# A fused sparse-attention and maxout kernel: fewer copies on GpSimd, another build of the distance table, another order of all units

## The chip, the cores and the metric

The kernel runs on one core of a Trainium2 chip. The metric is the time of one execution on the device, in microseconds. Three runs of the kernel before took 177.97, 178.1 and 178.21 us (median 178.1 us).

## What is computed

Inputs are q, k and v (4 batches, 8 heads, 768 positions, 64 per head, float32) and four weight matrices; the output is 3072 x 512 in float32.

```python
scores = scale * q @ k.T                       # per batch and head
keep   = (pos_k < 8) | (0 <= rel < 96)         # rel = pos_q - pos_k
dist   = where(global and not local, 96, |rel|)
scores = where(keep, scores - slope[h] * dist, -1e9)
a = softmax(scores);  x = concat_heads(a @ v)  # 3072 x 512
h = max(max(x @ w1, x @ w2), x @ w3)           # 512 -> 768
out = h @ w_out                                # 768 -> 512
```

A query sees the 96 positions up to its own and the first 8 positions of its batch. The slopes are 2^-1 to 2^-8 over the heads.

## The kernel before

The 3072 rows are 24 tiles of 128 queries, six to a batch. A tile works on a window of keys of its own and the tile before it (two sets of 128 keys, the global keys put into unused columns); the first tile of a batch has one set. Tiles come in seven chunks of 4, 2, 2, 4, 4, 4 and 4 for the two matrix layers, so a first-layer product is 512 or 256 columns wide.

The work is written as units, and the string SCHEDULE lists the units in the order in which they are issued. Each engine executes its part in that order, so the string fixes the order on every engine and on SP's DMA queue, and no scheduler changes it. A unit's last number often says which engine does its copy: 0 ScalarE (ACT), 1 VectorE (DVE), 2 GpSimd (POOL); in the transposes other numbers choose a pair of engines or a DMA. The units that matter here:

- l and v (load_part, load_v): load two tiles of Q or K, or of V, in float32, 512 KB. w and o load weight blocks. All but the first load of K are issued by SP.
- c (cast_part, L185) casts Q or K to bf16; C (cast_v, L188) casts half of a V pair; W (L489) and Q (L492) cast the weights.
- x (u_x): TensorE transposes of Q or K and the copy out of PSUM (L263 and L265; whole ones L282 and L284); how = 9 is a transpose by DMA (L249). In how 6 one half is copied by ScalarE and the other by VectorE, in 7 both by ScalarE, in 8 both by VectorE.
- Y (L192, L194): half copies of V into the key window's layout; Z (L205) copies the first keys; G (L230) and V (L192, L194) put the global keys and their V rows into the windows ("gathers" below).
- S (u_S): scores (L303) and their exponential on ScalarE (L314). For the first tiles a bias goes into the scores by a matmul (L296); for the others M (L330, L332) multiplies by a mask table on VectorE.
- A (u_A): product with V (L356) and division by the sums on VectorE (L360 to L369).
- T (u_XT): transposes of a tile's result (L397, L407, copies L400, L408), or by DMA (how = 4, L377).
- F (u_F1): one of three first-layer products (L420). F c.f.0 is copied by ScalarE (L425), F c.f.1 and F c.f.2 are a maximum on VectorE (L427, L429).
- O (u_F2) and E: second layer (L435), copy (L444), store.
- B and K build eight bias and eight mask tables from the distance table (L319 on ScalarE or VectorE; L323 on ScalarE). D issues dummy matmuls (L500).

PSUM has three buffers of one bank (psH) shared by F, O and some others, two double-bank score tiles (psS), and one bank for transposes (psT).

The distance table is built before the first unit: GpSimd counts positions into rbase (L509), VectorE makes the third set of keys, the condition and the maximum over all 384 columns (L514 to L521), and copies the table with its columns regrouped into rbq (L522). B reads rbq, K reads rbase.

Of the kernel before, what the change touches and what calls it, by code (L numbers as in the profile page):

```python
# [22 lines left out]


SCHEDULE = """
    D0.0 D7.0 D6.0 c0.0.2 D1.8 B0.0 B7.0 D9.4 D5.4 B3.1 B5.1 B4.1 l1.1 l1.0 c1.0.2 K3 K7 K4 K5 B1.0
    c0.1.1 x0.1.3 Z0.1 K1 B2.0 K6 B6.0 D3.4 K2 x0.0.6 S1.0.1 S1.1.1 G1.0 v0 C0.0.2 K0 c1.1.1 x1.1.8
    S0.0.1 x1.0.8 C0.1.2 Y1.0.1 S2.1.1 Y0.1.1 S2.0.1 G2.0 v1 V2.2 M1.0 M1.1 A1.2 Y0.0.1 M2.0 l2.0
    c2.0.1 C1.0.2 S0.1.1 M0.1 S3.0.1 M3.0 T1.8 C1.1.2 Y1.1.2 V3.2 S3.1.1 M3.1 G3.2 M0.0 A0.2 l2.1
    c2.1.2 x2.0.2 M2.1 A2.0 A3.1 Y2.0.2 T0.0 x2.1.7 T2.0 S4.0.1 w0.0 W0.0.2 w0.1 T3.8 l3.0 c3.0.1  # L30
    S4.1.0 M4.1 F0.0.0 W0.1.2 F0.0.1 G4.2 S5.0.0 S5.1.0 x3.0.8 F0.1.0 w0.2 V4.2 W0.2.2 M5.0 w1.0
    W2.0.0 v2 F0.0.2 C2.0.2 C2.1.2 W1.0.1 F0.1.1 F0.1.2 Y2.1.2 V5.2 M5.1 F0.2.0 F0.3.0 F0.4.0 w1.1
    W1.1.0 F0.5.0 W2.1.1 A5.0 M4.0 A4.1 F0.5.1 w1.2 W2.2.1 T5.0 F0.2.1 F0.4.1 T4.1 W1.2.0 l3.1
    F0.4.2 F0.5.2 c3.1.0 x3.1.6 Z1.2 l4.0 c4.0.0 F0.2.2 l4.1 v3 F1.2.0 F1.3.0 c4.1.1 l5.1 S7.0.0
    S6.1.0 C3.0.0 x4.0.6 C3.1.2 F1.2.1 F1.2.2 F1.4.0 F1.3.1 l5.0 o2 o1 F1.0.0 M7.0 o0 S7.1.0 S6.0.0
    c5.1.0 x4.1.6 v4 l7.0 F1.3.2 F1.4.1 l6.0 M7.1 F1.0.1 F1.4.2 v6 v5 F1.1.0 G7.2 A7.0 F1.5.0 F1.5.1
    l6.1 Q1.1 F1.1.1 F1.0.2 c5.0.0 S8.1.0 x5.0.6 S8.0.0 Q2.0 c7.0.0 Y3.0.0 F1.5.2 Q0.1 F0.3.1 M6.0
    F0.3.2 G8.2 Y3.1.2 Y4.0.2 M6.1 M8.0 F1.1.2 C4.0.1 l7.1 V8.2 S9.0.0 S9.1.0 G9.2 C4.1.2 x5.1.8
    O0.2.0 Y5.0.2 Y4.1.2 O1.0.0 C6.0.0 A6.0 O0.0.0 M9.1 T7.8 S10.1.0 S10.0.0 c6.0.0 c6.1.0 G10.0
    T6.8 M8.1 M9.0 V10.1 O1.1.1 M10.1 x6.1.9 C6.1.2 C5.0.2 V9.2 A8.1 Y7.0.2 F2.4.0 A9.0 x7.0.9  # L40
    F2.1.0 O0.1.0 M10.0 T9.4 F2.0.0 v7 T8.4 C5.1.0 l9.1 F2.4.1 S11.1.0 x6.0.8 S11.0.0 M11.1 Y5.1.2
    F2.1.1 F2.5.0 V11.2 O0.3.0 S13.1.0 c7.1.1 Z2.0 S13.0.0 x7.1.6 G13.1 F2.0.1 F2.0.2 l8.0 F2.5.1
    l9.0 l8.1 M11.0 F2.4.2 A10.1 F2.2.0 F2.2.1 A11.0 F2.3.0 F2.3.1 F2.5.2 F2.3.2 S12.0.0 T11.8 V14.2
    S12.1.0 F2.1.2 F2.2.2 S14.0.0 T10.6 S14.1.0 G14.2 Y6.0.0 O2.1.0 v9 M13.0 Y6.1.1 M14.0 F3.0.0
    M13.1 C7.0.1 C7.1.2 A13.1 F3.4.0 F3.1.0 M14.1 M12.1 c8.0.1 S15.1.0 S15.0.0 c8.1.0 Y7.1.1 v10
    T13.4 v8 Y8.0.1 O2.0.1 F3.3.0 F3.0.1 M15.1 F3.0.2 V15.0 C9.0.0 A14.1 V16.1 F3.1.1 M15.0 M12.0
    F3.2.0 F3.1.2 F3.4.1 F3.2.1 F3.3.1 F3.3.2 x8.0.9 x8.1.9 G15.2 c9.0.1 c9.1.0 x9.1.9 A12.0 C8.0.0
    C8.1.2 F3.5.0 F3.5.1 A15.1 F3.4.2 S16.0.0 x9.0.8 S16.1.0 M16.0 F3.2.2 F3.5.2 Z3.0 T15.6 G16.0
    l10.0 v11 T14.4 l10.1 S19.1.0 S19.0.0 O3.2.1 l11.1 O3.0.0 C10.0.2 C9.1.1 Y9.1.2 G19.2 Y8.1.2
    S17.1.0 T12.8 M19.1 S17.0.0 O3.1.0 M16.1 Y10.0.1 F4.1.0 A16.0 M17.0 F4.2.0 F4.0.0 c10.0.2  # L50
    x10.0.9 F4.0.1 c10.1.2 x10.1.9 F4.3.0 M19.0 M17.1 S18.1.0 S18.0.0 T16.4 l11.0 F4.0.2 A19.2 V17.2
    A17.1 F4.2.1 O3.3.0 T19.8 c11.1.0 S20.0.0 M18.1 M18.0 S20.1.0 G20.1 C11.0.1 F4.2.2 c11.0.2
    Y9.0.2 x11.0.9 C10.1.1 Y10.1.1 F4.4.0 F4.3.1 F4.5.0 A18.1 F4.1.1 F4.4.1 V20.0 S21.1.0 S21.0.0
    F4.4.2 G21.2 x11.1.9 C11.1.2 Y11.1.0 V23.0 F4.1.2 F4.5.1 T17.4 T18.4 F4.3.2 S22.1.0 M20.0 M20.1
    S22.0.0 G22.0 M22.1 F5.4.0 F5.4.1 F4.5.2 M21.1 F5.2.0 M21.0 A20.1 T20.4 F5.2.1 O4.2.1 F5.0.0
    F5.0.1 S23.0.0 M23.0 S23.1.0 F5.3.0 F5.2.2 V21.1 F5.1.0 M23.1 M22.0 F5.1.1 Y11.0.2 F5.3.1 V22.2
    A23.0 A22.2 T22.4 A21.1 O4.1.0 O4.3.0 T21.4 T23.4 F5.3.2 F5.4.2 F5.5.0 F5.5.1 O4.0.0 F5.0.2
    F5.1.2 F6.4.0 F6.1.0 F5.5.2 F6.1.1 F6.1.2 F6.3.0 F6.4.1 F6.4.2 F6.2.0 F6.5.0 F6.5.1 O5.0.0
    F6.5.2 F6.3.1 O5.1.1 O5.3.1 F6.0.0 F6.3.2 F6.2.1 F6.0.1 F6.2.2 F6.0.2 O5.2.0 E D4.1 D2.2 D8.0
"""  # L60


# [1 line left out]
def kernel(  # L64
# [437 lines left out]
    with tc.manual_schedule():  # L502
        load_part(0, 1)
        load_part(0, 0)

# [16 lines left out]
        nc.vector.tensor_copy(rbq.rearrange("p s (e i) -> p s e i", e=2), rbase.rearrange("p s (i e) -> p s e i", e=2))  # L522
# [43 lines left out]
```

## Time and profile before

| | |
|---|---|
| median of 3 runs | 178.1 us |
| the profiled execution | 178.15 us, of which the profile spans 176.4 us |
| busy: TensorE, VectorE, ScalarE, GpSimd | 169.0, 133.0, 109.2, 39.2 us |
| HBM read, written | 25.17 MB, 6.29 MB |
| TensorE clock granted | 1.0 |

The profile is one execution. Names of engines: PE is TensorE (PEld its weight loads), DVE VectorE, ACT ScalarE, POOL GpSimd, SP the engine that issues DMAs. Rows give line, engine, operation, output and inputs, count, busy microseconds and mean nanoseconds. Rows of stages give start and end, length, then busy time and count of PE, PEld, DVE, ACT and POOL, the clock, the DMA share and GB/s. Rows of the chain of waits give start, length and what stood on it. Rows in order of time give start, length, engine, line and operation. A few matmul records are missing.

### The profile page before, as it was taken

To read this page: it belongs to the slowest core of one execution; us is meant where nothing else is said; L and a number is where in the kernel's file an instruction comes from. 1 tells how busy PE (TensorE), PEld (TensorE's weight loads), DVE (VectorE), ACT (ScalarE), POOL (GpSimd) and SP (SyncE) were. 2 spreads that over 40 slices of the span, in tenths; PEclk is the share of its full clock that TensorE was granted. 3 is DMA by queue.
4 is the path that set the end of the run, shared out by engine and by line. 5 is a ranking of instruction groups with operands and counts; after the bars stand their busy time and mean duration, and the time that the engine had idled before them with its cause. 6 is when DMAs were issued, how large, how long until landed. Compare 5 with 4: busy or idle time off the path is not lost.

```text
span 176.4 us, 4322 instructions
## 1 busy us (share of the span) xinstructions
PE 169.0 (96%) x1695; PEld 94.0 (53%) x1717; DVE 133.0 (75%) x276; ACT 109.2 (62%) x170; POOL 39.2 (22%) x63
## 2 busy tenths in 40 slices
PE   7989899999999999999999999999999999999993
PEld 2445654558854668744545545444546444444452
DVE  7767796898999998996999598987969634534700
ACT  3998995769898988489625864669443222231042
POOL 2257845112076250020001280403000000000000
PEclk9999999999999999999999999999999999999999
DMA  4999999999999588999999398572030251003025
GB/s 126 346 309 331 364 350 382 385 351 383 288 290 302 192 207 180 278 299 277 228 227 284 88 259 144 164 152 30 0 89 4 59 149 61 4 32 117 29 92 205
DMA packets 53908, 35.54 MB, mean 201 GB/s; under 512 B 16768, under 2 KB 46336, under 8 KB 53888
## 3 DMA queue, kind: packets, MB, share of 16 engines
q1 hardware_dynamic: 52704, 34.68, 69.7%
q10 hardware_dynamic: 1184, 0.59, 1.2%
q8 instruction: 13, 0.21, 0.5%
q14 instruction: 7, 0.06, 0.1%
HBM read 25.17 MB, written 6.29 MB: 178 GB/s over the span
## 4 chain that ended last, share of the span: by engine, by line
PE 79%; DVE 8%; DMA 7%; POOL 2%; issue 2%; ACT 1%; SPq 0%; DVEq 0%
PE h L420 46%; PE po L435 15%; DMA rawv<-in_v_dram 7%; PE sp L303 5%; PE op L356 5%; PE wp L500 4%; DVE P L330 3%; PE tpr L258 2%; ACT P L314 1%; DVE qkT L265 1%; POOL vo L188 1%; DVE ht L429 1%; PE xtr L397 1%; DVE xT L400 1%; DVE wo L492 1%
## 5 line engine op out<-in xcount | busy, mean ns | idle before, releaser
L420 PE MATMUL h<-xT,w 128*128 128x512 bf16 (+1 forms) x492 | 99.4, 348 | 1.2 <-DVE xT L400 0.4
L420 PEld LDWEIGHTS <-w 128*128 128x128 bf16 x504 | 47.0, 98 | 41.5 <-issue 0.8
L314 ACT ACTIVATE P<-sp 128x1024 bf16<-128x1024 f32 (+1 forms) x48 | 43.7, 956 | 6.4 <-PE sp L303 5.9
L425 ACT CAST h<-h 128x512 bf16<-128x512 f32 (+1 forms) x42 | 22.0, 530 | 30.8 <-PE h L420 29.7
L435 PE MATMUL po<-wo,ht 128*128 128x512 bf16 (+2 forms) x146 | 33.2, 362 | 0.8 <-DVE ht L429 0.2
L429 DVE TENSOR_TENSOR ht<-h,h 128x512 bf16<-128x512 bf16 (+1 forms) x42 | 25.4, 608 | 10.4 <-PE h L420 8.9
L427 DVE TENSOR_TENSOR h<-h,h 128x512 bf16<-128x512 bf16 (+1 forms) x42 | 25.2, 606 | 9.1 <-PE h L420 8.5
L330 DVE TENSOR_TENSOR P<-P,wmask 128x1024 bf16<-128x1024 bf16 x33 | 23.8, 742 | 0.8 <-ACT P L314 0.6
L444 ACT COPY ost<-po 128x512 f32<-128x512 f32 (+2 forms) x19 | 10.5, 558 | 20.7 <-PE po L435 19.5
L435 PEld LDWEIGHTS <-ht 128*128 128x128 bf16 x156 | 14.3, 98 | 15.3 <-issue 0.5
L356 PEld LDWEIGHTS <-P 128*128 128x128 bf16 x352 | 13.2, 97 | 4.1 <-DVE P L330 0.7
L303 PE MATMUL sp<-qkT 64*128 64x128 bf16 x320 | 13.9, 217 | 0.5 <-DVE qkT L265 0.4
L369 DVE TENSOR_TENSOR xb<-op,rz 128x512 bf16<-128x512 f32 x20 | 13.8, 692 | 0.7
L303 PEld LDWEIGHTS <-qkT 64*128 64x128 bf16 x320 | 9.3, 94 | 8.1 <-issue 5.3
L185 POOL CAST qkp<-rawp 128x1024 bf16<-128x1024 f32 x6 | 7.4, 1248 | 15.0 <-DMA rawp<-in_q_dram 14.9
L444 DVE COPY ost<-po 128x512 f32<-128x512 f32 (+1 forms) x7 | 4.4, 632 | 8.1 <-PE po L435 8.1
L185 ACT CAST qkp<-rawp 128x1024 bf16<-128x1024 f32 x10 | 10.4, 1052 | 0.0
L188 POOL CAST vo<-rawv 128x512 bf16<-128x512 f32 x10 | 6.9, 702 | 15.5 <-DMA rawv<-in_v_dram 10.7
L500 PE MATMUL wp<-zeros 128*128 128x512 bf16 x23 | 7.9, 508 | 1.2 <-DVE zeros L513 1.2
L230 POOL COPY qkT<-qkT 128x32 bf16<-128x32 bf16 x9 | 2.5, 278 | 25.7 <-PE sp L303 16.9
L265 DVE COPY qkT<-tpr 128x512 bf16<-128x512 bf16 x11 | 7.3, 685 | 0.7 <-PE tpr L258 0.5
L192 POOL COPY ve<-vo 64x520 int32<-64x520 int32 x8 | 5.5, 684 | 5.1 <-ACT vo L188 3.4
(86 smaller groups left out, 137.3 us busy)
## 6 DMA issues: line engine op xcount, KB each, us to landing
rawv<-in_v_dram SPq DMA_DIRECT2D x12, 512.0 KB, 6.9
out_dram<-ost SPq DMA_DIRECT2D x23, 256.0 KB, 2.3
rawp<-in_k_dram SPq DMA_DIRECT2D x8, 512.0 KB, 6.4
rawp<-in_q_dram SPq DMA_DIRECT2D x12, 256.0 KB, 6.6
wst<-in_moe_w_dram SPq DMA_DIRECT2D x3, 1024.0 KB, 10.6
rawp<-in_q_dram SPq DMA_DIRECT2D x6, 512.0 KB, 8.1
wst<-in_moe_w_dram SPq DMA_DIRECT2D x3, 512.0 KB, 8.6
rawp<-in_k_dram SPq DMA_DIRECT2D x6, 256.0 KB, 8.6
```

Of the source, the lines that this page charges most:

```text
L185: copies[how](qk, src)
L303: nc.tensor.matmul(sp[:, z, i, ds], k_cols(T, hsl, jp, ds), q_cols(T, hsl, jp), start=not how, stop=True, skip_group_check=True)
L314: nc.scalar.activation(dst, src, AF.Exp, bias=0.0, scale=scale)
L330: nc.vector.tensor_mul(P, P, wmask[:, g, :, 0:2])
L356: nc.tensor.matmul(o, P[:, i, ds], vs[ds][:, h], start=(ds == 0), stop=(ds == len(vs) - 1), skip_group_check=True)
L420: nc.tensor.matmul(ps, w123[f // 2][:, dm, j, (f % 2) * 128:(f % 2) * 128 + 128], xT[c][:, dm], start=(dm == order[0]), stop=(dm == order[ ...
L425: nc.scalar.copy(h01, ps)
L427: nc.vector.tensor_max(h01s[c, f], h01s[c, f], ps)
L429: nc.vector.tensor_max(ht[c][:, f], h01s[c, f], ps)
L435: nc.tensor.matmul(po, ht[c][:, f, tt * 128:(tt + 1) * 128], wo[:, f, cols], start=(f == 0), stop=(f == NF - 1))
L444: copy(ost, po)
L500: nc.tensor.matmul(wp, zeros[:, 0:128], zeros, start=True, stop=True)
```

## The change

1. In SCHEDULE, the engine numbers of many units are different. GpSimd has 15 of the 56 copies, casts and gathers that it had: 4 of 6 casts of Q or K, 5 of 14 casts of V, 2 of 13 half copies Y, 2 of 10 gathers V, 2 of 3 weight casts, and none of the 9 gathers G or the key copy Z. All but two of them stand ahead of the first F unit. ScalarE and VectorE take the others, and work is moved between these two as well (outputs O on VectorE 9 in place of 6; transposes x copied by both or by ScalarE more often). Transposes by DMA are 22 in place of 20.
2. All units stand in a new order. The dummy matmuls are 21 in place of 23, none of them behind E.
3. The distance table is made in one layout, rbq, which K reads with a step. Two selects on GpSimd make the first two sets; VectorE makes only the third.

```diff
-    rbase = persist.tile([128, 3, 128], FP32, name="rbase")
+    rbq = persist.tile([128, 3, 128], FP32, name="rbq")
...
-        nc.scalar.activation(wmask[:, g, 2 * z + i], rbase, AF.Exp, bias=0.0, scale=-slopes[h])
+        nc.scalar.activation(wmask[:, g, 2 * z + i].rearrange("p s (i e) -> p s e i", e=2),
+                             rbq.rearrange("p s (e i) -> p s e i", e=2), AF.Exp, bias=0.0, scale=-slopes[h])
...
-        rbq = stage_pool.tile([128, 3, 128], FP32, name="rbq", tag="wst0")
-        rtmp = stage_pool.tile([128, 3, 128], FP32, name="rtmp", tag="wst0")
-        nc.gpsimd.iota(rbase[:, 0:2], base=128, pattern=[[-1, 2], [1, 128]], channel_multiplier=-2,
+        dist = stage_pool.tile([128, 2, 2, 64], FP32, name="dist", tag="wst0")
+        rtmp = stage_pool.tile([128, 128], FP32, name="rtmp", tag="wst0")
+        nc.gpsimd.iota(dist, base=128, pattern=[[-1, 2], [1, 2], [2, 64]], channel_multiplier=-2,
...
+        near, own = rbq[:, 0:2].rearrange("p s (e i) -> p s e i", e=2), rbq[:, 2]
+        nc.gpsimd.affine_select(out=near, in_=dist, compare_op=ALU.is_ge, fill=BIGD, base=128,
+                                pattern=[[-1, 2], [1, 2], [2, 64]], channel_multiplier=-2)
+        nc.gpsimd.affine_select(out=near, in_=near, compare_op=ALU.is_ge, fill=BIGD, base=NL - 129,
+                                pattern=[[1, 2], [-1, 2], [-2, 64]], channel_multiplier=2)
...
-        nc.vector.scalar_tensor_tensor(out=rtmp, in0=rbase, scalar=1.0 - NL, in1=rbase, op0=ALU.add, op1=ALU.mult)
+        nc.vector.scalar_tensor_tensor(out=rtmp, in0=own, scalar=1.0 - NL, in1=own, op0=ALU.add, op1=ALU.mult)
...
-        nc.vector.tensor_tensor(out=rbase, in0=rbase, in1=rtmp, op=ALU.max)
+        nc.vector.tensor_tensor(out=own, in0=own, in1=rtmp, op=ALU.max)
...
-        nc.vector.tensor_copy(rbq.rearrange("p s (e i) -> p s e i", e=2), rbase.rearrange("p s (i e) -> p s e i", e=2))
```

The orders around the first units of the first layer, before and after, show how the string changes:

```
before: w0.0 W0.0.2 w0.1 T3.8 l3.0 c3.0.1 S4.1.0 M4.1 F0.0.0 W0.1.2 F0.0.1 G4.2 S5.0.0 S5.1.0 x3.0.8 F0.1.0 w0.2 V4.2 W0.2.2 M5.0 w1.0 W2.0.0 v2 F0.0.2
after:  w0.0 W0.0.0 l3.0 w0.1 S4.0.1 M4.0 T3.8 V4.2 W0.1.2 S4.1.0 D7.1 G4.0 w0.2 F0.1.0 F0.0.0 S5.1.0 c3.0.1 x3.0.6 M4.1 w1.0 W1.0.0 S5.0.0 F0.1.1 W0.2.2 F0.1.2
```

More of the change, by code (lines that the diff above doesn't have):

```diff
@@ L31 @@
[L31 to L42, printed above, removed]
@@ L49 @@
[L49 to L54, printed above, removed]
@@ new lines @@
+    V5.1 F0.5.0 w1.1 W1.1.0 W2.1.1 F0.4.0 A4.1 A5.0 F0.5.1 T4.0 F0.4.1 w1.2 W1.2.0 l3.1 T5.1 F0.2.1
+    F0.2.2 l4.0 c4.0.1 W2.2.0 F0.5.2 c3.1.0 x3.1.7 Z1.0 F0.4.2 F1.0.0 F1.2.0 l4.1 c4.1.1 S7.0.0
+    S6.1.0 l5.0 x4.0.6 l5.1 o0 F1.0.1 F1.0.2 c5.0.1 M7.0 F1.3.0 F1.4.0 F1.4.1 o2 c5.1.1 x4.1.7
+    S6.0.0 S7.1.0 G7.0 v3 F1.2.1 F1.2.2 F1.3.1 Q2.1 F0.3.1 M7.1 Q0.0 F1.5.0 F1.5.1 S8.0.0 x5.0.7
+    S8.1.0 G8.1 C3.0.2 C3.1.1 Y4.0.1 F0.3.2 F1.5.2 A7.0 F1.4.2 F1.1.0 M6.0 x5.1.6 v5 o1 Q1.0 v4
+    S9.0.0 S9.1.0 l7.0 l6.1 C5.0.1 C5.1.0 F1.1.1 F1.3.2 Y3.1.1 M8.0 F1.1.2 T7.0 v6 l6.0 M6.1 v7
@@ new lines @@
+    Y3.0.1 M9.0 O0.2.1 l7.1 C4.0.0 O0.0.0 G9.0 V8.1 A6.1 c7.0.1 M8.1 c6.1.1 x6.1.9 O0.3.0 C4.1.0
+    Y4.1.1 O0.1.1 Y5.1.0 S10.1.0 T6.8 V9.1 M9.1 S10.0.0 O1.0.0 A8.1 M10.1 T8.4 F2.0.0 x7.0.9 G10.0
+    F2.4.0 c6.0.0 l8.1 v9 l9.1 F2.0.1 F2.1.0 M10.0 F2.0.2 S11.0.0 c7.1.0 Y5.0.1 x6.0.6 S11.1.0 V10.1
+    F2.1.1 M11.0 F2.4.1 C6.0.0 A9.0 F2.2.0 V11.1 l9.0 O1.1.1 S13.1.0 x7.1.6 S13.0.0 G13.0 M11.1
+    F2.2.1 F2.1.2 C6.1.1 F2.2.2 A11.1 F2.3.0 F2.5.0 A10.0 Y6.1.0 Z2.0 F2.4.2 T11.0 F2.5.1 F2.3.1
+    C7.0.0 S12.1.0 T9.8 S12.0.0 F2.3.2 v8 C7.1.1 F2.5.2 M12.0 S14.1.0 T10.6 S14.0.0 c8.1.0 O2.0.0
@@ new lines @@
+    l8.0 M13.0 G14.1 Y7.1.1 M12.1 F3.2.0 V15.0 M13.1 c9.1.1 x9.1.9 F3.0.0 Y7.0.1 A13.1 F3.3.0 l11.1
+    T13.4 M14.0 x8.1.9 M14.1 F3.0.1 S15.1.0 Y6.0.0 S15.0.0 F3.3.1 F3.3.2 F3.1.0 M15.0 M15.1 V14.0
+    F3.4.0 c8.0.1 c9.0.0 x9.0.9 l10.0 F3.0.2 A12.1 F3.2.1 x8.0.9 C9.0.0 C8.0.0 A14.0 F3.1.1 T12.4
+    l10.1 G15.1 Y8.0.1 c11.1.0 O2.1.0 A15.1 F3.5.0 F3.1.2 C9.1.1 F3.2.2 T15.8 S19.0.0 M19.0 S19.1.0
+    c10.0.0 T14.4 C8.1.0 Y8.1.0 F3.4.1 l11.0 v10 F3.5.1 F3.5.2 F3.4.2 Y10.0.1 M19.1 Z3.1 S16.0.0
+    S16.1.0 G16.1 V20.0 O3.3.0 O3.2.1 A19.1 F4.5.0 c10.1.1 x10.1.9 v11 F4.1.0 V16.1 G19.1 x10.0.9
@@ new lines @@
+    Y9.0.1 S18.1.0 S17.0.0 M17.0 M16.1 F4.3.0 F4.3.1 F4.5.1 M16.0 V17.1 F4.1.1 S17.1.0 S18.0.0
+    F4.2.0 Y9.1.0 O3.0.0 M18.0 M17.1 C10.0.1 M18.1 A16.1 F4.1.2 T19.4 O3.1.1 A18.0 A17.1 C11.0.1
+    c11.0.0 x11.0.9 F4.0.0 F4.2.1 F4.2.2 F4.3.2 T18.4 S20.1.0 S20.0.0 T16.4 T17.4 x11.1.9 C10.1.1
+    Y10.1.1 F4.0.1 G20.1 F4.0.2 F4.5.2 S21.0.0 S21.1.0 G21.0 M20.0 F4.4.0 F4.4.1 C11.1.1 F4.4.2
+    M21.1 F5.1.0 F5.2.0 V21.1 O4.2.1 F5.3.0 Y11.1.0 F5.3.1 M20.1 S22.0.0 S22.1.0 F5.2.1 F5.5.0
+    Y11.0.0 F5.2.2 V23.1 F5.4.0 A20.1 F5.3.2 M22.0 M21.0 G22.0 S23.0.0 M23.0 S23.1.0 T20.4 F5.5.1
@@ L60 @@
+    O4.1.1 A21.1 T21.4 M23.1 M22.1 O4.0.0 V22.0 F5.4.1 F5.0.0 A23.1 T23.4 O4.3.0 A22.0 F5.4.2 F5.5.2
+    F5.0.1 F5.1.1 F5.0.2 T22.4 F5.1.2 F6.3.0 F6.5.0 F6.4.0 F6.5.1 F6.4.1 F6.4.2 O5.1.0 F6.3.1 F6.1.0
+    O5.3.1 F6.1.1 F6.0.0 F6.0.1 F6.0.2 O5.0.1 F6.2.0 F6.2.1 F6.3.2 O5.2.0 F6.2.2 F6.1.2 F6.5.2 E
+    D6.0
 """
@@ L513 @@
         nc.vector.memset(zeros, 0.0)
-        nc.vector.tensor_scalar_add(rbase[0:64, 2], rbase[0:64, 0], -128.0)
-        nc.vector.tensor_scalar_add(rbase[64:128, 2], rbase[64:128, 0], -1.0)
-        nc.vector.scalar_tensor_tensor(out=rtmp, in0=rbase, scalar=1.0 - NL, in1=rbase, op0=ALU.add, op1=ALU.mult)
+        near, own = rbq[:, 0:2].rearrange("p s (e i) -> p s e i", e=2), rbq[:, 2]
[3 more added lines that the diff above has]
+                                pattern=[[1, 2], [-1, 2], [-2, 64]], channel_multiplier=2)
+        dist0 = dist[:, 0].rearrange("p e i -> p (e i)")
+        nc.vector.tensor_scalar_add(own[0:64], dist0[0:64], -128.0)
+        nc.vector.tensor_scalar_add(own[64:128], dist0[64:128], -1.0)
+        nc.vector.scalar_tensor_tensor(out=rtmp, in0=own, scalar=1.0 - NL, in1=own, op0=ALU.add, op1=ALU.mult)
         nc.vector.tensor_scalar(out=rtmp, in0=rtmp, scalar1=0.0, scalar2=BIGD, op0=ALU.is_gt, op1=ALU.mult)
-        nc.vector.tensor_tensor(out=rbase, in0=rbase, in1=rtmp, op=ALU.max)
-        nc.vector.memset(rbase[0:NG // 2, 0:2], float(NL))
+        nc.vector.tensor_tensor(out=own, in0=own, in1=rtmp, op=ALU.max)
         for row in (0, 64):
-            nc.vector.tensor_scalar_min(rbase[row:row + NG // 2, 2], rbase[row:row + NG // 2, 2], float(NL))
-        nc.vector.tensor_copy(rbq.rearrange("p s (e i) -> p s e i", e=2), rbase.rearrange("p s (i e) -> p s e i", e=2))
+            nc.vector.tensor_scalar_min(own[row:row + NG // 2], own[row:row + NG // 2], float(NL))
+        nc.vector.memset(rbq[0:NG // 2, 0:2], float(NL))
         make_identity(nc, identb)
```

23 lines of the change are left out of this document (7 added, 16 removed).

## The prediction

> **What bounds the kernel now.** I read the page's first two parts, then busy time by stages, then the chain of waits, and last the rows at the places where the chain leaves TensorE.
>
> ```profile
> span 176.4 us, 4322 instructions
> PE 169.0 (96%) x1695; PEld 94.0 (53%) x1717; DVE 133.0 (75%) x276; ACT 109.2 (62%) x170; POOL 39.2 (22%) x63
> PE 79%; DVE 8%; DMA 7%; POOL 2%; issue 2%; ACT 1%; SPq 0%; DVEq 0%
> ```
>
> TensorE is busy for 96% of the span and holds 79% of the chain. None of its useful work is removed, so a gain must come from places where it waits. The stages say where:
>
> ```profile
> 25.00:76.00 51.00, 50.07 (x641) 33.59 (x648) 46.36 (x97) 41.30 (x65) 15.21 (x24) 1.00 0.98 296
> 33.00:41.00 8.00, 8.00 (x90) 4.79 (x89) 7.50 (x15) 5.73 (x9) 1.32 (x2) 1.00 1.08 367
> 41.00:49.00 8.00, 8.00 (x131) 6.85 (x130) 7.41 (x17) 7.38 (x14) 0.65 (x3) 1.00 1.08 325
> 49.00:57.00 8.00, 7.55 (x83) 3.98 (x84) 7.70 (x15) 7.47 (x12) 5.58 (x10) 1.00 1.11 291
> 57.00:65.00 8.00, 7.82 (x125) 5.72 (x122) 7.55 (x19) 7.40 (x13) 2.46 (x4) 1.00 0.67 193
> ```
>
> The columns after the length are PE, PEld, DVE, ACT and POOL. From 25 to 76 us VectorE is busy 46.36 of 51.0 us, 91%. With VectorE at 94% (7.50 of 8) and 93% (7.41) TensorE lost nothing; at 94% with ScalarE at 93% it lost 0.18; where VectorE stood at 96% and GpSimd had its most work (5.58 us) it lost 0.45. So the kernel is bound by TensorE, with VectorE close behind it between 25 and 76 us, and that stretch decides this change.
>
> There the chain leaves TensorE at these rows:
>
> ```profile
> 49.57 0.97 DVE wo L492
> 52.40 1.01 DVE P L330
> 101.08 2.27 DVE P L330 x2
> ```
>
> and in order of time the same places, with what GpSimd did beside them, read:
>
> ```profile
> 47.29 0.69 DVE L492 CAST wo<-wost 128x1024 bf16<-128x1024 f32 x1
> 49.37 1.64 POOL L192 COPY ve<-vof 64x520 int32<-64x520 int32 x2
> 49.48 1.05 DVE L492 CAST wo<-wost 128x1024 bf16<-128x1024 f32 x1
> 51.99 0.88 POOL L188 CAST vo<-rawv 128x512 bf16<-128x512 f32 x1
> 52.32 1.09 DVE L330 TENSOR_TENSOR P<-P,wmask 128x1024 bf16<-128x1024 bf16 x1
> 75.47 0.74 DVE L192 COPY vf<-vof 64x260 int32<-64x260 int32 x1
> 101.42 2.82 POOL L185 CAST qkp<-rawp 128x1024 bf16<-128x1024 f32 x2
> L330 DVE TENSOR_TENSOR P<-P,wmask x33: 670/685/1518, 23.3 to 134.6; 128x1024 bf16<-128x1024 bf16 x33
> ```
>
> The same cast takes VectorE 0.69 us alone and 1.05 us beside a GpSimd copy; the mask product has a median of 0.685 us, but 1.09 beside a GpSimd cast, and up to 1.518 in the pair at 101 us. Instructions of VectorE that read and write SBUF stretch when GpSimd runs. These stretched instructions stand on the chain.
>
> The Trainium skill, "SBUF — State Buffer", section "Who interferes with whom", explains such rows: VectorE and GpSimd share one pair of ports as an exclusive lock, and a multiplication with both inputs in SBUF collides with GpSimd's reads. The trace agrees (0.685 against 1.518 us).
>
> **The change, part by part.**
>
> *Order at the start: 0.* The distance table is built in a shorter chain.
>
> ```profile
> masks.py:199 POOL TENSOR_SCALAR_AFFINE_SELECT identb<-identb 128x128 bf16<-128x128 bf16 x1 | 0.3, 292 | 0.1
> 4.66 0.94 ACT L319 ACTIVATE bias<-rbq 128x384 bf16<-128x384 f32 x2 [1.98 <-DVE rbq L522]
> 23.91 1.04 POOL L489 CAST w<-wst 128x1024 bf16<-128x1024 f32 x1 [1.10 <-DMA wst<-in_moe_w_dram]
> 25.00 0.27 PEld L420 LDWEIGHTS <-w 128*128 128x128 bf16 x2 [0.16 <-POOL w L489]
> ```
>
> ScalarE waited 1.98 us for the table, until 4.66 us. Two selects of 256 elements cost GpSimd between 0.29 us each (the row's 128 elements) and twice that; three VectorE steps shrink from 384 to 128 elements and a copy goes, so I take the table 0.5 to 1.5 us earlier. But TensorE comes to the third weight block only at 25.0 us, and that block was cast from 23.91 on, as soon as its DMA landed. In the new order the queue holds the same loads ahead of it, GpSimd still casts it, and TensorE still has exactly three units of the first layer (then F0.0.0, F0.0.1, F0.1.0; now F0.1.0, F0.0.0, F0.1.1), the same score and transpose units and the attention of tiles 0 to 3 ahead of that point. Whatever the table saves is waited off there: 0. If the cover is gone (a later GpSimd cast of tile pair 1, both of whose casts it now has, or ScalarE's new copy between the exponentials of tiles 2 and 3, about 1 us), it costs up to 1 us; I keep 0 to +1. The stepped read of the mask tables is ScalarE's and lies in the same cover. The two dummy matmuls fewer: three of 23 stood behind the last product, at the end, beside the last stores; 0.
>
> *The stretch from 25 us to the first unit of chunk 3 (75.9 us).* By the orders this stretch holds, in both kernels, 51 first-layer units, 18 score units, 8 attention products, 7 outputs and 9 transposes of Q and K: TensorE's work is the same to 0.3 us. What changes is who copies. Prices of VectorE and ScalarE here:
>
> ```profile
> L185 DVE CAST qkp<-rawp 128x1024 bf16<-128x1024 f32 x2 | 1.5, 728 | 0.0
> L188 DVE CAST vo<-rawv 128x512 bf16<-128x512 f32 x1 | 0.4, 418 | 0.0
> L192 DVE COPY ve<-vo 64x520 int32<-64x520 int32 x3 | 1.3, 425 | 0.1
> L444 DVE COPY ost<-po 128x512 f32<-128x512 f32 x1 | 0.7, 671 | 0.0
> L265 DVE COPY qkT<-tpr 128x512 bf16<-128x512 bf16 x8 | 5.3, 684 | 0.3 <-PE tpr L258 0.3
> L400 DVE COPY xT<-xtr 128x256 bf16<-128x256 bf16 x7 | 1.7, 283 | 0.2 <-PE xtr L397 0.2
> L489 DVE CAST w<-wst 128x1024 bf16<-128x1024 f32 x3 | 2.3, 753 | 1.5 <-DMA wst<-in_moe_w_dram 1.5
> L492 DVE CAST wo<-wost 128x1024 bf16<-128x1024 f32 x2 | 1.7, 870 | 0.0
> L330 DVE TENSOR_TENSOR P<-P,wmask 128x1024 bf16<-128x1024 bf16 x13 | 9.7, 750 | 0.1
> L185 ACT CAST qkp<-rawp 128x1024 bf16<-128x1024 f32 x7 | 7.3, 1052 | 0.0
> L188 ACT CAST vof<-rawv 128x512 bf16<-128x512 f32 x2 | 1.2, 624 | 0.0
> L265 ACT COPY qkT<-tpr 128x512 bf16<-128x512 bf16 x4 | 2.4, 591 | 1.5 <-PE tpr L258 1.5
> ```
>
> VectorE gains four casts of Q or K (4 x 0.728 = 2.9), three of V (3 x 0.418 = 1.25), five half copies of V (5 x 0.425 = 2.1) and one small one (0.3), four gathers of V's global rows (priced as the half copies, 4 x 0.425 = 1.7), two outputs (2 x 0.671 = 1.3), a gather of K (0.2) and one mask product that slips in (0.7): 10.4 us. It loses one weight cast (0.75) and one of the output weights (0.87), four long copies of transposed Q or K (2.7) and one short (0.4), two of transposed rows (0.6): 5.3 us. Net +5.1 us. With GpSimd down from 24 instructions to one in this stretch, the collisions go: 13 x (0.750 - 0.685) = 0.85 for the mask products, 2 x (0.87 - 0.69) = 0.35 for the output weights, 0.45 for the copy at 75.47 (0.74, where I take 0.3 from the 0.425 of a copy of twice its length), 0.2 for the weights: 1.9 us. VectorE then needs 46.36 + 5.1 - 1.9 = 49.5 us where it had 51.0.
>
> ScalarE gains four casts of V, five copies of transposed Q or K, two of transposed rows and one key copy at 0.6 (7.2 us), two weight casts at 1.05 (2.1), three gathers of K at 0.2 and 0.4 on half copies, and loses three casts of 1.05 and two outputs of 0.6: +6.0, to 47.3 us.
>
> So the stretch can't be shorter than 49.5 us (-1.5), if VectorE never idles. At the share of the fullest window, 96%, it is 51.5 us (+0.5); with TensorE's loss in that window (7.55 of 8, 94%) it is 50.07 / 0.944 = 53.0 us (+2.0). That last window's loss stands at two collisions (0.36 and 0.40 us too long) that are gone afterwards, and at 93% with both engines full TensorE lost nothing. I therefore take 98% for VectorE: 50.6 us, -0.4.
>
> The Trainium skill, "Perfetto Trace Analysis", section "Optimizing Scalar/DVE Operations", speaks on both sides: where VectorE is saturated it allows moving work to ScalarE or even GpSimd, but says that a move between VectorE and GpSimd might not help, for the shared port. By its first half the change goes the wrong way in this stretch, which is the second rival below; by its second half moving work back costs little, which is what 98% says.
>
> *After 76 us.*
>
> ```profile
> 81.00:89.00 8.00, 7.95 (x52) 3.90 (x51) 6.56 (x13) 6.10 (x9) 0.78 (x1) 1.00 1.24 262
> L330 DVE TENSOR_TENSOR P<-P,wmask 128x1024 bf16<-128x1024 bf16 x12 | 9.0, 772 | 0.0
> ```
>
> VectorE has air there (6.56 of 8 us from 81 us on; the second row is the mask products from 75 to 120 us). The pair at 101 us (2.27 us on the chain against 1.37 for two medians) delays the second product by 0.9 us, but TensorE had other work beside it: from 0 to -0.9, and I take -0.15. GpSimd's gathers of K, on which score units wait, go to VectorE and ScalarE at 0.2 us: 0.
>
> *End.*
>
> ```profile
> xT<-xb SPq DMA_TRANSPOSE x11, 3.2
> 161.21 5.18 PE h L420 x24
> ```
>
> The transpose of tile 22 is now the last, with six first-layer units between the attention product that feeds it and the first unit that reads it. Six such units are 24 matmuls, 5.18 us by the chain; a transpose by DMA lands 3.2 us after its issue, which leaves 2 us for the division before it. Covered: 0; up to +1 if VectorE is late there.
>
> **Sum.** 0 - 0.4 - 0.15 + 0 = -0.55 us on the profiled execution's own 178.15 us (span 176.4 and 1.75 us around it), which stands at the median of the runs, 178.1: 177.6 us.
>
> **The rivals.**
>
> *More gain.* VectorE stays full to the end of the stretch (49.5 us, -1.5), and stalls later shrink too, for which the mask products of 75 to 120 us speak, 12 x (0.772 - 0.685) = 1.0 us at most: 178.15 - 1.5 - 1.0 = 175.7. For it: the chain stands on stretched instructions. Against it: no window of 8 us shows VectorE above 96%.
>
> *Slower: VectorE becomes the bound.* Same place, 25 to 76 us. Two engines at 95% and 92% hand work to each other in order (exponential, product, attention, copy), three PSUM buffers deep, and TensorE waits as it did from 49 to 57 us. It decides as soon as VectorE's share falls below 97% (49.5 / 51.0): at 96% it gives 178.15 + 0.5 - 0.15 = 178.5, with TensorE's share of that window 180.0. For it: that window, and no GpSimd to overflow to. It is about as well supported as my forecast.
>
> *No difference.* The relief of 1.9 us and the added 5.1 us meet with VectorE at 96.2 to 97.6% of the stretch (51.5 to 50.7 us): within 0.2% of 178.1.
>
> *The stretching isn't GpSimd's.* If VectorE's long instructions have another cause, the relief is 0, VectorE needs 46.36 + 5.1 = 51.5 us, and the stretch grows to at least that: 178.5 to 180.5. The pairs of rows above speak against it.
>
> *Start uncovered:* +0.5 to +1, 178.6 to 179.1.
>
> **How the numbers follow.** 0.2% is 0.36 us, about what a measurement of this kernel can tell from no change. Chances: forecast (176.9 to 177.7) 0.28, more gain (175 to 176.9) 0.20, no difference 0.15, VectorE bound 0.28, another cause 0.04, start uncovered 0.05. So faster 0.48, same 0.15, slower 0.37. Most likely single case: 177.6, own range 176.9 to 177.7; as both signs hold much, the range for 8 in 10 goes from 175.6 to 180.1.
>
> **What would show it.** In the changed kernel's profile: GpSimd near 15 us busy with nothing after about 40 us; the mask products' longest near 0.7 us instead of 1.518; the third weight block still cast near 23.9 us and read at 25; the first unit of chunk 3 starting at 75.5 us, with VectorE at 98% before it. If that unit starts after 76.3 us with VectorE waiting often for TensorE and ScalarE, the VectorE rival is right. If it starts before 75 us, the gain is larger. If the third block is read before 24 us or after 26 us, my reading of the start is wrong. What would make it all wrong is a wait that no row of before holds: a load that comes too late for its buffer, or a transposed tile at the end.

## The result and the profile after

The changed kernel takes 176.84 us (median; 176.77 to 177.49), the kernel before 178.1 us (177.97 to 179.15), 11 runs each. The ratio is 0.9926, 95% interval 0.9905 to 0.9946: 1.3 us faster, where 177.6 us was forecast. The profiled execution took 176.79 us (before: 178.15).

The first part of its page and the first line of the chain:

```profile
span 175.0 us, 4237 instructions
...
PE 168.7 (96%) x1687; PEld 92.8 (53%) x1687; DVE 133.6 (76%) x288; ACT 120.0 (69%) x188; POOL 14.2 (8%) x24
...
PE 90%; ACT 6%; DVE 2%; issue 1%; POOL 0%; POOLq 0%; ACTq 0%
```

GpSimd went from 39.2 to 14.2 us, ScalarE from 109.2 to 120.0, VectorE only from 133.0 to 133.6. TensorE holds 90% of the chain in place of 79%.

The stages that the prediction showed (columns as there: PE, PEld, DVE, ACT, POOL):

```profile
25.00:76.00 51.00, 50.95 (x649) 33.67 (x648) 48.55 (x109) 46.38 (x78) 0.62 (x1) 1.00 1.08 309
33.00:41.00 8.00, 8.00 (x90) 4.80 (x89) 7.08 (x14) 6.72 (x11) 0.00 (x0) 1.00 1.04 382
41.00:49.00 8.00, 7.95 (x121) 5.85 (x119) 7.66 (x17) 7.58 (x15) 0.62 (x1) 1.00 1.16 311
49.00:57.00 8.00, 8.00 (x91) 5.09 (x88) 7.89 (x21) 6.67 (x12) 0.00 (x0) 1.00 0.95 253
57.00:65.00 8.00, 8.00 (x127) 5.74 (x126) 7.84 (x18) 7.94 (x13) 0.00 (x0) 1.00 1.06 300
65.00:73.00 8.00, 8.00 (x132) 6.17 (x128) 7.90 (x21) 7.64 (x15) 0.00 (x0) 1.00 1.18 238
```

The last row is the window behind the prediction's. In the fourth row VectorE is busy 7.89 of 8 us (99%), in the fifth ScalarE 7.94 (99%) beside VectorE's 7.84, and in both TensorE is busy all 8 us. The mask products are even, by the view of their line:

```profile
L332 DVE TENSOR_TENSOR P<-P,wmask x33: 670/684/693, 25.0 to 137.0; 128x1024 bf16<-128x1024 bf16 x33
```

The longest is 0.693 us, where it was 1.518.

**A trap in the profile of before.** Its page counts 1695 matmuls but 1717 weight loads (PE and PEld in the second line that the prediction quotes); the changed kernel's counts 1687 of each. So 22 matmul records are missing there, 8 of them in the stretch from 25 to 76 us: a product of the second layer reads "x5" where the code issues 6. Each of these 8 leaves a hole of 0.05 us that looks like a wait, 0.42 us of the 0.93 us that TensorE is not busy there. The weight loads are complete, so I measure TensorE by them. Such loads of the two layers follow each other every 0.216 us when nothing holds them. These are its loads, in order of time, at the boundaries of the prediction's steps, first before, then after: the third weight block, chunk 3's first unit, and E.

```profile
25.00 0.92 PEld L420 LDWEIGHTS <-w 128*128 128x128 bf16 x5 [0.16 <-POOL w L489]
75.73 0.74 PEld L420 LDWEIGHTS <-w 128*128 128x128 bf16 x4
166.01 6.71 PEld L435 LDWEIGHTS <-ht 128*128 128x128 bf16 x42
```

```profile
24.51 1.41 PEld L422 LDWEIGHTS <-w 128*128 128x128 bf16 x8
75.85 1.61 PEld L422 LDWEIGHTS <-w 128*128 128x128 bf16 x8
166.02 0.10 PEld L437 LDWEIGHTS <-ht 128*128 128x128 bf16 x1
```

Before, the third block is read from 25.00 us on. After, the first row holds four loads of another block and then four of the third. It ends at 24.51 + 1.41 = 25.92 us, the last load takes 0.10 us, and the first of the four starts three distances before it: 25.92 - 0.10 - 3 x 0.216 = 25.17 us. Before, the last row holds six loads of one output unit ahead of the 36 of E: E starts at 166.01 + 6 x 0.216, 167.30 us by its own record.

| part | before | after | difference | forecast |
|---|---|---|---|---|
| start, to the third weight block | 25.00 | 25.17 | +0.17 | 0 |
| to chunk 3's first unit | 50.73 | 50.68 | -0.05 | -0.4 |
| to E | 91.57 | 90.17 | -1.40 | -0.15 |
| E to the end of the span | 9.07 | 8.96 | -0.11 | 0 |
| sum (of the unrounded parts) | 176.4 | 175.0 | -1.40 | -0.55 |

At chunk 3's first unit the changed kernel is 0.12 us behind the kernel before (75.85 against 75.73 us). The whole gain comes after it.

**What the 1.40 us are.** Part of it is work. TensorE's loads between chunk 3's first unit and E, grouped by line, have these rows before:

```profile
L397 PEld LDWEIGHTS <-xb 64*128 64x128 bf16 x24 | 0.6, 95 | 0.8 <-issue 0.8
L258 PEld LDWEIGHTS <-qkp 64*128 64x128 bf16 x16 | 0.3, 95 | 0.0
```

and only this one after:

```profile
L399 PEld LDWEIGHTS <-xb 64*128 64x128 bf16 x8 | 0.2, 94 | 0.4 <-DVE ht L431 0.4
```

Thirty-two transposes are gone from this part: 16 of Q or K and 16 of the rows, because two more tiles are transposed by DMA and because transposes stand earlier. At the spacing that such loads have when nothing holds them (0.014 and 0.020 us) that is 16 x 0.014 + 16 x 0.020 = 0.55 us. The rest, 1.40 - 0.55 = 0.85 us, is waiting that went. I compared the distance of each two successive loads with the usual distance of such a pair in the two traces. Before, five distances after 25 us are over 0.2 us too long: at 31.0 (0.44), 53.2 (0.39), 57.2 (0.29), 77.0 (0.56) and 103.1 (0.30). After, there are three: 46.4 (0.29), 59.7 (0.31) and 72.6 (0.20), none behind 76 us. (In those at 31.0 and 59.7, 0.19 us is no waiting: behind a 512-column product of the layers the second load of an attention product comes that much later in every other place of both traces too.) The two late ones of before (0.86 us together) read, among TensorE's loads in order of time:

```profile
77.58 0.30 PEld L356 LDWEIGHTS <-P 128*128 128x128 bf16 x8 [0.49 <-DVE P L330]
...
103.39 0.30 PEld L356 LDWEIGHTS <-P 128*128 128x128 bf16 x8 [0.23 <-DVE P L330]
```

TensorE had done half of an attention product and waited for the second mask product of the tile. In the changed kernel the same product runs through, all 16 loads in one row. A second unit of the first layer stands ahead of it (eight loads from 75.85 us on, where before there were four from 75.73), so it starts only at 77.58 us, when the mask products are done:

```profile
77.58 0.74 PEld L358 LDWEIGHTS <-P 128*128 128x128 bf16 x16
```

### The profile page after: what moved, and what is told of

Its sections match the earlier page's. It is cut to its first block, busy times and chain, and to the rows that moved or that the text cites. A ratio compares the mean times of both kernels' runs of the same rounds, so it can differ in the third digit from the quotient of the medians.

```text
span 175.0 us, 4237 instructions
## 1 busy us (share of the span) xinstructions
PE 168.7 (96%) x1687; PEld 92.8 (53%) x1687; DVE 133.6 (76%) x288; ACT 120.0 (69%) x188; POOL 14.2 (8%) x24
## 3 DMA queue, kind: packets, MB, share of 16 engines
HBM read 25.17 MB, written 6.29 MB: 180 GB/s over the span
## 4 chain that ended last, share of the span: by engine, by line
PE 90%; ACT 6%; DVE 2%; issue 1%; POOL 0%; POOLq 0%; ACTq 0%
PE h L422 53%; PE po L437 18%; PE sp L304 7%; PE op L358 6%; PE tpr L259 2%; ACT wmask L324 2%; PE sp L297 2%; ACT qkT L266 1%; PE xtp L409 1%; ACT bias L320 1%; PE oph L358 1%; ACT wo L494 1%; ACT P L315 1%; PE xtr L399 0%; DVE qkT L266 0%
## 5 line engine op out<-in xcount | busy, mean ns | idle before, releaser
L332 DVE TENSOR_TENSOR P<-P,wmask 128x1024 bf16<-128x1024 bf16 x33 | 22.0, 683 | 2.0 <-ACT P L315 1.9
L446 ACT COPY ost<-po 128x512 f32<-128x512 f32 (+2 forms) x16 | 8.8, 554 | 15.8 <-PE po L437 15.3
L371 DVE TENSOR_TENSOR xb<-op,rz 128x512 bf16<-128x512 f32 x22 | 15.2, 692 | 0.8
L446 DVE COPY ost<-po 128x512 f32<-128x512 f32 (+1 forms) x10 | 6.5, 647 | 8.4 <-PE po L437 8.4
L186 DVE CAST qkp<-rawp 128x1024 bf16<-128x1024 f32 x12 | 8.1, 686 | 0.9 <-DMA rawp<-in_k_dram 0.9
L186 ACT CAST qkp<-rawp 128x1024 bf16<-128x1024 f32 x8 | 8.4, 1050 | 0.0
L266 DVE COPY qkT<-tpr 128x512 bf16<-128x512 bf16 x6 | 4.0, 688 | 4.5 <-PE tpr L259 4.5
L266 ACT COPY qkT<-tpr 128x512 bf16<-128x512 bf16 x12 | 6.6, 588 | 1.0 <-PE tpr L259 1.0
L370 DVE RECIPROCAL rz<-op 128x8 f32<-128x8 f32 x22 | 4.4, 199 | 2.1 <-PE op L358 1.9
L259 PE MATMUL tpr<-identb,qkp 64*128 64x64 bf16 x208 | 5.4, 190 | 0.2 <-DVE qkT L266 0.2
```

What stands on the lines that cost most here:

```text
L186: copies[how](qk, src)
L332: nc.vector.tensor_mul(P, P, wmask[:, g, :, 0:2])
L371: nc.vector.tensor_tensor(out=x.rearrange("p (g h) d -> p g h d", g=2), in0=o4[:, :, :, 0:64], in1=rz[:, :, :, None].to_broadcast([128, 2, ...
L446: copy(ost, po)
```

## The experiments

The theory after the result: the gain is the new order, with the engines that it was laid out for; GpSimd's collisions are a small part, since what their end relieves comes back as added load. The rival: GpSimd's collisions are what the kernel lost, and fewer copies there bring the gain in any order.

### GpSimd's later copies put back

All units and the table as after, but the 39 units behind the third weight block that had left GpSimd are on it again.

```diff
-... C2.0.0 C2.1.0 ... Y2.1.1 V5.1 ... Z1.0 ... G7.0 ... c10.0.0 ... V22.0 ...
+... C2.0.2 C2.1.2 ... Y2.1.2 V5.2 ... Z1.2 ... G7.2 ... c10.0.2 ... V22.2 ...
```

> The changed kernel with its order and table, but the 39 copies, casts and gathers behind the third weight block that GpSimd had before are GpSimd's again. Theory (collisions): VectorE's SBUF instructions stretch again beside GpSimd (longest mask product over 1 us in place of 0.693) and TensorE waits for them: 177.5 to 178.2 us against 176.84. Rival (the order alone made the gain, who copies matters little): 176.7 to 177.0. Second rival (VectorE's and ScalarE's load is what costs, so taking 5 us off them helps): below 176.6.

Measured: 177.32 us (176.71 to 177.44), ratio 0.994 [0.9912, 0.9967]. GpSimd works 38.6 us (39.2 before the change), VectorE 131.2, ScalarE 109.9, and a mask product is stretched to 1.1 us again, by the view of its line:

```profile
L332 DVE TENSOR_TENSOR P<-P,wmask x33: 674/683/1096, 25.7 to 137.5; 128x1024 bf16<-128x1024 bf16 x33
```

The median lies between the two ranges that were expected. Three of nine runs take 176.71 to 176.75 us, as little as the changed kernel's shortest; where the others lose 0.6 us is told below. The profile is of one of the others (177.33 us), and by the boundaries of the table its loss is at the start alone: the third block is read at 25.80 us in place of 25.17, and the parts behind it take 50.47, 90.27 and 9.00 us, 139.7 us together as against 139.8. The product at 78 us runs through all the same, and no load behind 76 us is over 0.2 us late:

```profile
77.99 0.74 PEld L358 LDWEIGHTS <-P 128*128 128x128 bf16 x16
```

So the collisions as such cost next to nothing in the new order, and the stops at 77 and 103 us are gone although GpSimd works as much as before the change.

### The engines without the order

The order and the table of before, with those 39 units on the engines that they have after.

```diff
-... C2.0.2 ... Y2.1.2 ... V5.2 ...   (before's order)
+... C2.0.0 ... Y2.1.1 ... V5.1 ...
```

> The kernel before, with its order and table, but the same 39 units on the engines that the changed kernel gives them. Theory (collisions): the waits at 50 to 53, 76 to 77 and 101 to 103 us shrink, 177.0 to 177.5 against 178.1. Rival (the order): the old order was laid out with GpSimd as a third engine, so VectorE and ScalarE are late at more places: 178.1 or longer.

Measured: 189.48 us, ratio 1.0658 [1.0609, 1.0706], 11.6 us slower than before: its rival (178.1 or longer) was right. TensorE's waits, by line (total, times, longest):

```profile
PE op L357 <- DVE vo L193: 3.9, 2, 2.0
PE op L357 <- ACT P L315: 1.4, 1, 1.4
```

Attention products wait for copies of V on VectorE, whose place in the queue was chosen for GpSimd.

### The order without the engines

The order and the table of after, with every engine number of before.

> The changed kernel's order and table with every unit's engine as before. Theory (the order makes the gain): 176.7 to 177.4, the gain stays. Rival (order and engines fit only together): over 178.1.

Measured: 198.81 us, ratio 1.1137 [1.1091, 1.1183]. That the order alone keeps the gain was a miss. The first waits are for casts at the start:

```profile
PE tpr L259 <- POOL qkp L186: 2.7, 1, 2.7
PE tpp L280 <- DVE qkp L186: 1.9, 1, 1.9
```

In the old order the fewer copies on GpSimd cost 11.6 us, and with the old engines the new order takes 20.9 us more than the kernel before. The rival is refuted from both sides. What made the gain is the new order together with the rest of its engine choices, most of them between ScalarE and VectorE, which the first experiment kept; no run gives all the new engines to the old order, or parts these two.

### Extra GpSimd copies, and extra memsets

The changed kernel, with GpSimd made to work beside the 39 copies that it gave away: behind each it copies 128x512 of zeros into a scratch tile that nothing reads, or, in the second kernel, only fills it (memset in place of the diff's last line).

```diff
+        nc.gpsimd.tensor_copy(scr1[0:made.shape[0]], made)
+        nc.gpsimd.tensor_copy(scr, zeros)
```

> The changed kernel, and after each of those 39 units GpSimd waits for its output (a copy of one column) and copies 128x512 bf16 of zeros to a scratch tile that nobody reads. VectorE's and ScalarE's work is the same and nothing waits for GpSimd, so only collisions can cost. Theory: mask products and casts stretch, 177.2 to 177.9 against 176.84. Rival (collisions cost nothing here): within 0.2 us of 176.84.

> As the extra copies, but GpSimd fills the scratch tile with zeros in place of copying, so beside the one column it reads nothing from SBUF. If the collision is between reads (as the Trainium skill, SBUF - State Buffer, Who interferes with whom, has it for instructions with two SBUF inputs), the mask products don't stretch and the time stays within 0.2 us of 176.84; if GpSimd's writes collide as well, as much is lost as with the copies, 177.2 to 177.9.

Measured: 180.25 us, ratio 1.0109 [1.0077, 1.0141], with copies, and 180.11 us, ratio 1.0104 [1.0071, 1.0136], with memsets: over 2 us above both expectations. VectorE's busy time grew by 4.6 and 2.8 us. The mask products and VectorE's casts of Q and K (minimum, median, maximum in ns), with copies:

```profile
L334 DVE TENSOR_TENSOR P<-P,wmask x33: 670/682/898, 25.5 to 140.4; 128x1024 bf16<-128x1024 bf16 x33
L188 DVE CAST qkp<-rawp x12: 680/686/1509, 5.8 to 104.4; 128x1024 bf16<-128x1024 f32 x12
```

with memsets:

```profile
L334 DVE TENSOR_TENSOR P<-P,wmask x33: 667/683/693, 25.6 to 140.3; 128x1024 bf16<-128x1024 bf16 x33
L188 DVE CAST qkp<-rawp x12: 681/686/1123, 5.6 to 104.2; 128x1024 bf16<-128x1024 f32 x12
```

The cast of 1509 ns, at 22.2 us, ran beside GpSimd's cast of a weight block; beside the extras the longest is 1097 ns with copies and 1123 with memsets. A GpSimd that reads SBUF stretches both; one that, but for a column, only writes it leaves the mask products alone and still stretches the casts. The Trainium skill, "SBUF — State Buffer", section "Who interferes with whom", says both: an instruction with two SBUF inputs contends with GpSimd's reads and not with its writes, while copies and casts can take both ports. These rows agree. The time was the same in both, so the mask products aren't what cost it. Part of it is no collision. By the boundaries of the table 0.42 and 0.60 us are lost ahead of the third block, where the extras haven't begun (the stop at 20 us, below), and 2.8 and 2.7 us from there to chunk 3. In that stretch GpSimd's own last cast of V stood behind the extras, and with copies VectorE and TensorE waited for it (1.19 and 0.35 us). So 2.8 us is an upper bound for collisions in that stretch, where VectorE is busy 7.87 and 7.90 of 8 us in two windows (98 and 99%). In the first experiment VectorE has as much to do in one window (7.97 of 8 us from 57 to 65 us) but not over the stretch: 46.20 of 51 us, where the changed kernel has 48.55.

### The table alone, in either order

> The changed kernel with the distance table built as before (two layouts, no selects). If what the start saves is waited off before the first layer's third weight block (the prediction), within 0.2 us of 176.84. Rival: ScalarE's eleven tables stand on the chain from 3.83 to 8.93 us, so a table that is ready 0.8 us later costs up to 0.8 us: 177.3 to 177.7.

> The kernel before with the new distance table alone. If the start is waited off, within 0.2 us of the kernel before; if the table is part of the gain, 0.4 to 0.9 us faster.

Measured: after with before's table 177.41 us (177.1 to 177.66), ratio 0.9956 [0.9939, 0.9974]; before with the new table 178.12 us, ratio 1.0002 [0.9978, 1.0026]. In the old order the table is worth nothing. In the new one it looked like 0.6 us, but the trace says otherwise. TensorE in order of time, with the old table:

```profile
18.99 0.48 PE L357 MATMUL op<-vo,P 128*128 128x65 bf16 x10
20.07 0.36 PE L357 MATMUL op<-vo,P 128*128 128x65 bf16 x6 [0.60 <-issue]
```

and in the changed kernel:

```profile
19.13 0.66 PE L358 MATMUL op<-vo,P 128*128 128x65 bf16 x16
```

With the old table TensorE comes to tile 3's product 0.14 us earlier. After the 10th of 16 matmuls it stands still for 0.60 us, for nothing that the profile shows. The first experiment's profile and those of the extra copies and memsets have the same stop at the same matmul (0.46, 0.26 and 0.43 us), always ending near 20.0 us (19.85 to 20.07); the changed kernel's profile, taken from a run of 176.79 us, has none. Its eleven runs lie at 176.77 to 176.84 (seven) and 177.36 to 177.49 (four). So I asked whether the stop belongs to the product or to a place in TensorE's stream of instructions.

### The stop at 20 us

Three kernels from the changed one: 12 dummy matmuls fewer at the start, the same dummies cut into 24 of half the width, and, for the start's remaining wait, one gather on VectorE.

```diff
-D0.4 D4.4 ... D5.4        +D0.0 D4.0 ... D5.0     (fewer)
-D0.4 D4.4 ... D5.4        +D0.8 D4.8 ... D5.8     (more: each 256 columns wide)
-G4.0                      +G4.1                   (gather)
```

> The changed kernel without the 12 dummy matmuls of its first three D units (24 instructions of TensorE fewer ahead of everything). In four earlier variants TensorE stands still for 0.26 to 0.60 us after the 10th of 16 matmuls of tile 3's product, until about 20.0 us, for nothing that the profile shows; the changed kernel's runs lie at 176.8 or at 177.4. Theory: the stop belongs to a place in TensorE's instruction stream, and what it waits for comes at about 20 us. Then it moves 24 instructions later in the work, behind that product and into the transposes that follow; TensorE comes there some 0.4 us later and stops for 0.2 us at most: nearly all runs at 176.7 to 177.0. Rival: it belongs to the product (a wait for data that the profile doesn't show): it stays at the 10th matmul, and the runs lie at 176.8 and 177.4 as before. Other rival: the dummies keep the clock up, the first matmuls take longer, and all runs lie above 177.

> The changed kernel with those 12 dummy matmuls of 512 columns made 24 of 256 columns (as many columns, 24 instructions of TensorE more ahead of everything). If the stop belongs to a place in the instruction stream, it moves 24 instructions earlier in the work, to the transposes of a row tile ahead of tile 3's product or the product's first two matmuls; TensorE comes there some 0.4 us earlier and stops up to 1.0 us: runs at 176.8 where nothing stops it and up to 177.8 where it does, the median at or above 177.4. If it belongs to the product, it stays at the 10th matmul with 176.8 and 177.4.

> The changed kernel with one gather of K (tile 4's, G4) on VectorE in place of ScalarE. In the changed kernel tile 5's scores wait 0.42 us for it at 23.7 us, since ScalarE's queue holds it behind an exponential and a weight cast. If what the start loses is carried to the end, because TensorE waits for nothing after 47 us, this gives 0.2 to 0.4 us: 176.4 to 176.6 without the stop at 20 us, 177.0 with it. Rival: VectorE's row of work there is as late, or the third weight block (cast by 24.4 us) takes the wait's place: within 0.1 us of 176.8 and 177.4.

With 24 instructions more, 176.77 us in all of six runs (176.73 to 176.80), ratio 0.9915 [0.9886, 0.9944]: the runs at 177.4 are gone, and so is the stop. That it belongs to a place in the stream is right; that it would come earlier and last longer is a miss. The gather on VectorE gave 177.36 us (176.82 to 177.61) with the stop in its profile (0.51 us at the same matmul), the shortest run as before. These are its rival's times, but for neither of the rival's reasons: the score loads come 0.52 us behind the first-layer load ahead of them with the gather on either engine, so nothing had waited for it. With fewer dummies 177.42 us (176.99 to 178.9): no stop in the profile, but the other rival came true, all runs but one lying above 177. The first transposes and bias products in its trace,

```profile
6.26 1.04 PE L280 MATMUL tpp<-identb,qkp 128*128 128x128 bf16 x8 [3.15 <-DVE qkp L186]
...
9.02 1.06 PE L297 MATMUL sp<-bias,identb 128*128 128x512 bf16 x2
```

take twice what they take with the dummies there (0.61 and 0.60 us in the kernel with more of them), until 12.5 us; TensorE then runs 1.1 us behind to the end (177.88 us in the profiled run). The Trainium skill, "TensorE: Matmul & The Clock Gate", section "What's actually happening", has the array at half its clock until it has been busy for about 3.4 us. The doubled durations agree, though here they last for some 6 us, and the column of the granted clock stands at 1.00 all the while.

The last run joins the old table to the 24 instructions more.

> The changed kernel with the distance table of before, and with the 24 dummy matmuls of 256 columns, with which no run of the changed kernel stood at the upper level (176.73 to 176.80 in six runs). With the old table alone the median was 177.41. If the 0.6 us of that run was the stop of TensorE in the middle of tile 3's product, and not the table, this gives 176.7 to 176.9, no stop there, and the table is worth 0.1 us or less. If the table is worth half a microsecond of the start, carried to the end, it gives 177.2 to 177.5 again.

Measured: 176.81 us (176.67 to 176.86), ratio 0.9918 [0.9895, 0.9941], and no stop. Against 176.77 us with the new table, the table is worth nothing in the new order either. What TensorE waits for at 20 us isn't fully settled. The Trainium skill, "Runtime: NRT & Kernel Launch", section "Instruction fetch mechanics", says that an engine's instructions come by DMA in blocks of 256 and that the crossing is mostly hidden; 444 instructions of TensorE stand ahead of the stop (222 matmuls, 222 loads), waits not counted, while 16 DMA engines are full. A block that comes late would explain it, and the traces show one. The page of the changed kernel counts 13 packets of instructions on DMA queue q8 (packets, MB, share of the 16 DMA engines' time):

```profile
q8 instruction: 13, 0.21, 0.5%
```

That is 16 KB each, and one for about 260 of TensorE's 3374 matmuls and loads, so these are most likely TensorE's. In the five profiles with the stop the first of them in the span starts at 17.41 to 17.59 us, after 170 to 180 weight loads, and lands at 18.52 to 18.70; TensorE goes on 1.3 to 1.5 us after that. In the changed kernel's own profile it starts after 152 loads and lands at 17.41 us. With the 24 instructions more it lands at 16.32 us, and with the old table besides at 16.11. With fewer dummies it lands at 19.57 us, but there TensorE itself is 1.1 us late. Every trace fits. That TensorE waits for just this block, and why it is sent later in some runs, no run shows.

### A shorter start

Three moves that I took for an improvement: the mask tables K1, K3 and K5 later, one transpose copied by VectorE alone, the gather as above.

```diff
-K1 K3 K5 c1.1.2 B7.0 x0.0.7 ... K4 ... G4.0
+c1.1.2 B7.0 x0.0.8 ... K4 K1 K3 K5 ... G4.1
```

> The changed kernel with a start that takes three mask tables out of ScalarE's way until after the first exponentials, copies the first transposed Q on VectorE, and puts tile 4's gather of K on VectorE, which sat idle there. If the first layer's start hangs on ScalarE's chain and not on the landing of weights, the third weight block is read 0.5 to 1 us earlier and the time falls to 175.9 to 176.5; if landings take it back, within 0.2 us of 176.84.

Measured: 178.81 us (177.4 to 179.18), ratio 1.0024 [0.9999, 1.005]: a miss. The tables now stand between the exponentials of ScalarE, by its rows in order of time:

```profile
11.96 1.02 ACT L315 ACTIVATE P<-sp 128x1024 bf16<-128x1024 f32 x1 [0.70 <-PE sp L304]
12.88 0.21 ACT L231 COPY qkT<-qkT 128x32 bf16<-128x32 bf16 x1
12.99 2.06 ACT L324 ACTIVATE wmask<-rbq 128x384 bf16<-128x384 f32 x4
14.91 2.62 ACT L315 ACTIVATE P<-sp 128x512 bf16<-128x512 f32 x3
```

The third weight block is read 2.1 us later than in the changed kernel (27.28 in place of 25.17), and E's outputs end 2.1 us later too. A delay of the start isn't waited off anywhere: the parts behind it take 50.65, 90.17 and 8.97 us here, where the changed kernel's take 50.68, 90.17 and 8.96.

## Why the prediction was right or wrong

*What bounds the kernel.* Right: TensorE, with VectorE close behind from 25 to 76 us. The size of TensorE's loss there was read too large: the idle time of the stretch fell from 0.93 to 0.05 us, but the stretch, with 0.28 us more work, became only 0.05 us shorter. So 0.33 us of waiting went; of the 0.93, 0.42 are the holes of 8 missing matmul records.

*Start: 0.* For the table it held in both orders (178.12 against 178.1, 176.81 against 176.77). The reason, "whatever the table saves is waited off" at the third weight block, is not what happens in the changed kernel: the block is cast by 24.4 us and read at 25.17, so nothing waits for it. The new order itself is 0.17 us later, inside the 0 to +1 that was kept for it. That holds for the profiled run; a run with the stop at 20 us, as four of the eleven seem to be, starts some 0.6 us later still, and the prediction has no such term.

*The stretch: -0.4.* Measured -0.05, with 0.28 us more of TensorE's work in it (eight transposes of 0.055 us for eight of 0.020). VectorE was busy 48.55 us of 51.0, where 49.5 were forecast: it lost five long copies of transposed Q or K where four were counted (0.7 us), and the casts shed their collisions as well (0.686 us each, where the forecast took 0.728; 0.25 us), which had been left out. The assumption of 98% held in three windows running (7.84 to 7.90 of 8 us from 49 to 73 us), with TensorE busy all the time. But VectorE's work hardly sets the stretch's length: it takes 50.68 us with 48.55 us of it, and 50.47 with 46.20 in the first experiment.

*After 76 us: -0.15.* This is the step that failed, by its size: measured -1.40. Only the one pair of products at 101 us was priced. There were 0.30 us of waiting there, 0.56 us more at 77 us, just behind the boundary that had been drawn, and 0.55 us of TensorE's own work. The premise "none of its useful work is removed" was wrong: the transposes that go to DMA had been counted and given no price.

*End: 0.* Measured -0.11, with the three dummies behind E gone. The transpose of tile 22 was covered.

*The sum.* 176.84 us is 0.06 us below the forecast's own range (176.9 to 177.7) and inside the range for 8 in 10. That it was faster, as forecast, is in part luck: the term that made most of the -0.55 measured next to nothing, and the gain came from one that was put at -0.15.

*The rivals.* "More gain" has the right size for a partly wrong reason: 176.84 us lies in its share of the range, and its later stalls were there (0.86 us, where it allowed 1.0 at most), but its 1.5 us in the stretch were not. "No difference" is right for the stretch alone. "VectorE becomes the bound" is refuted in the changed kernel (99% from 49 to 57 us, and TensorE busy throughout); in the old order the same engines do make TensorE wait for VectorE (3.9 us in the largest row; 189.48 us in all). "Another cause of the stretching" is refuted by the extra copies. "Start uncovered" came true in part, +0.17.

*The main argument* was that stretched instructions on the chain made the gain. Putting the copies back on GpSimd kept the gain in its shortest runs. The order did it, with the other engine choices that go with it.

## What to carry to other kernels

Here a fixed order and its choice of engines were one thing, and each lost 11 us or more with the other's old version: price them together. Before you read a loss of TensorE out of a window, compare its matmuls with its weight loads, and measure by the loads. Where TensorE has next to no waits later on, every tenth of a microsecond of the start is carried to the end, and TensorE's work that is taken out must be priced as well.
